# Other token blocks for the first of two MLP layers behind an attention: 512, 256, 512, 512, 512

## Chip, cores and metric

One core of a Trainium2 chip runs the whole program. The metric is the device time in microseconds (us) of one execution; the time of a kernel is the median of its runs. PE is the matmul engine (TensorE), PEld its weight loads, DVE, ACT and POOL are VectorE, ScalarE and GpSimd, and SP issues the DMA transfers (SPq is its queue).

## What is computed

The input is an attention with 4 batches, 8 heads, 576 positions and head size 64, followed by two MLP layers over 2304 tokens, 512 -> 2048 -> 512 each, all in 32-bit floats.

```python
scores = scale * np.matmul(q, k.transpose(0, 1, 3, 2))
bias = -(cum[:, :, :, None] - cum[:, :, None, :])          # cum: running sum of max(s, 0)
scores = np.where(causal, -1e9, scores + np.minimum(bias, 0.0))
attn = softmax(scores)
x = (attn @ v), heads side by side: 2304 x 512
h = x @ w_in;  x = (h * np.clip(h + 3.0, 0.0, 6.0) / 6.0) @ w_out
h = x @ w2_in; out = (h * np.tanh(softplus(h))) @ w2_out
```

## The kernel before

**A planner writes the order.** Every piece of work is a node: engines that may run it, a cost, what it depends on, a due time (its priority) and the buffers that it takes. `Plan.run` (L124) walks through a modelled time, gives each engine the most urgent node that is ready and whose buffers are free, and then emits the instructions in that order. So each engine and SP's one DMA queue run a fixed order. Due times come from the table `T` (L34) in a unit in which one step of a 512-token block is 4: `pos` (L838) is where a step of the MLP stands, 64 for each 512-token block of 16 steps.

**Attention.** Two heads are worked on at a time, a pair. The first 256 positions of a batch are a `small` pair (L582 on): scores L610, score-and-bias minimum on DVE L622, exponential on ACT L629, row sums L637 and L638, scaling L647 and L649, transposes L655, copies L290, probabilities times V L664. Its result is split into a high and a low half and written from PSUM straight into the block of x in SBUF (L673, and L674 on DVE). The other 320 positions are a `unit` (L417 on): scores L486, L493, L501, transposes L532, PV L555, a split into staging tiles (L558 to L561), and a store to DRAM tensors `xs` (L568). `token` (L44) orders the tokens: the four first parts are tokens 0 to 1023, the four second parts are 1024 to 2303, 320 each. `FIRST` (the first parts of batches 0 and 1) runs ahead of everything; the other six parts come at the due times p0 to p5, spread over s0 to s5: first parts of batches 2 and 3, then second parts of batches 0, 1, 2 and 3.

**MLP.** Tokens are cut into five blocks, the same for both layers: 512, 512, 384, 512, 384. A block runs 16 steps f over the hidden size. GEMM1 (L722) is 12 matmuls into one bank: four chunks c of the input size, three products each, because weights and activations are held as a high and a low half. The gate follows (layer 1: ACT L733, DVE L735; layer 2: ACT L740), the split of its result (L290 and DVE L743), and GEMM2 (L755 in layer 1, L760 in layer 2), 12 matmuls per step in layer 1. `T["la"]` and `T["la2"]` say how many steps ahead GEMM1 falls due.

**Weights.** They arrive as 64-bit words and are made into two 32-bit halves by `load_split` (L328): one pass on ACT or DVE (L339, L341), DVE passes L345, L349 and L355, a copy, and a subtraction L365. Layer 1's w_in stays in 16 buffers `win`. w_out is split during block 0, stored to DRAM (`wos`, L390), and read again for each step of the later blocks (L393) into three buffers `wo`. Layer 2's w_out stays in 16 buffers that take the room of the attention's tiles once that is over.

**Blocks of x.** There are two buffers `blk`. Blocks 0 and 1 of layer 1 (tokens 0 to 1023) are taken at the start and filled by the attention from PSUM. Blocks 2 to 4 are loaded from `xs` (L697) once a buffer is free. Layer 1's output is scaled (L778), stored to DRAM tensors `ys` (L782) per block and 128 columns, loaded again by layer 2 (L700) and split (L372).

Of the kernel before, what the change touches and what calls it, by code (L numbers as in the profile page):

```python
# [24 lines left out]
NBLK = len(BLOCKS)  # L25
FIRST = [(0, 0, 2), (1, 0, 2)]
# [219 lines left out]
def tile_attention_moe_moe(ctx, tc, qk1, qk, v1, s, w_in, w_out, w2_in, w2_out, out):  # L246
    nc = tc.nc

    def r(ap):
        return ap.bitcast(F32)  # L250
# [25 lines left out]
    cuml = dr.tile([NB * NH, CTOT - 384], F32, name="cuml")  # L276
    xs = [[dr.tile([P, 2, n], F32, name=f"xs{i}_{c}") for c in range(NCC)] for i, (_, n) in enumerate(BLOCKS)]
    ys = [[dr.tile([P, n], F32, name=f"ys{i}_{c}") for c in range(NCC)] for i, (_, n) in enumerate(BLOCKS)]
    wos = [dr.tile([P, 2, DM], F32, name=f"wos{f}") for f in range(NF)]
# [89 lines left out]
    def split(dep, prio, buf, dst, n):  # L369
        h, l = dst  # L370
        a = add(("ACT", "DVE"), (act(n), v2x(n)), lambda e: copy(e, h(), r(l())), [dep], prio, (), [buf])
        return a, add("DVE", v1x(n), lambda: nc.vector.tensor_tensor(  # L372
            out=l(), in0=r(l()), in1=r(h()), op=ALU.subtract), [a], prio, (), [buf])
# [50 lines left out]
    def unit(b, h, prio, step, dep0, depc, banks):  # L424
# [138 lines left out]
        t0 = token(b, q0)  # L563
        for i, (b0, bn) in enumerate(BLOCKS):
            a, e = max(t0, b0), min(t0 + nq, b0 + bn)
# [6 lines left out]
    def small(b, h, pair, prio, step, dep0, depc, banks, fi, n_c1, n_id):  # L572
# [68 lines left out]
        for g in range(2):  # L641
# [11 lines left out]
            def tr(ps=ps, g=g):  # L653
                for z, o in ((0, 0), (P, P), (2 * P, 2 * P)):
# [13 lines left out]
        i, o = divmod(token(b, 0), 512)  # L668
        c, xb = h // 2, blk[0, i]
# [17 lines left out]

    ys_n = {(i, c): [] for i in range(NBLK) for c in range(NCC)}

    def load_block(layer, i, prio):  # L690
        n = BLOCKS[i][1]
        t = Buf(main_p, "blk", [P, NCC, 2, n], F32R)
        blk[layer, i] = t
        src_n = (xs_n, ys_n)[layer]
        for c in range(NCC):
            if layer == 0:
                ld = add("SP", 0.5, lambda c=c: nc.sync.dma_start(out=r(t.t)[:, c], in_=xs[i][c][:]),  # L697
                         src_n[i, c] + ([first] if c else []), prio, [t] if c == 0 else [], [t], lat=dma(P * n * 8))
            else:
                ld = add("SP", 0.5, lambda c=c: nc.sync.dma_start(out=r(t.t)[:, c, 1, :], in_=ys[i][c][:]),  # L700
                         src_n[i, c] + ([first] if c else []), prio, [t] if c == 0 else [], [t], lat=dma(P * n * 4))
            if c == 0:
                first = ld
            if layer == 0:
                blk_n[layer, i, c] = [ld]
                continue
            blk_n[layer, i, c] = split(ld, prio, t, (lambda c=c: t.t[:, c, 0, :], lambda c=c: t.t[:, c, 1, :]), n)

# [4 lines left out]
    def moe_step(layer, n, t1, t2, hb):  # L713
        i, f = divmod(n, NF)
        N = BLOCKS[i][1]
        x, w = blk[layer, i], win[layer, f]
# [53 lines left out]
    def y_out(layer, i, j, dep, prio):  # L770
        t0, N = BLOCKS[i]
        ps = ypst[layer, i][j]
        if layer == 0:
            t = Buf(main_p, "st", [P, 512], F32)

            def ev(e):
                if e == "ACT":
                    nc.scalar.activation(out=t.t[:, 0:N], in_=ps.t[:, 0:N], func=AF.Copy, scale=1.0 / 6.0)  # L778
                else:
                    nc.vector.tensor_scalar(out=t.t[:, 0:N], in0=ps.t[:, 0:N], scalar1=1.0 / 6.0, scalar2=None, op0=ALU.mult)  # L780
            a = add(("ACT", "DVE"), (actp(N), v1x(N)), ev, [dep], prio, [t], [ps])
# [14 lines left out]
    with tc.manual_schedule():  # L796
# [132 lines left out]
```

## Time and profile before

| | us |
|---|---|
| median of 3 runs | 1002.32 (1001.36 to 1003.06) |
| the profiled execution | 1003.14 |
| its span in the profile | 1001.4 |
| PE busy | 982.1 |
| DVE busy | 462.4 |
| ACT busy | 476.9 |

The span runs from the first to the last instruction in the trace. Matmuls are pipelined, so "busy" counts PE as soon as one is in flight; how close PE is to its pace is read from the start-to-start times of its matmuls. Layer 1 ends and layer 2 begins at about 600 us.

### The profile page before, as it was taken

What the parts mean: (1) busy time and instruction counts of PE and PEld (TensorE: products, weight loads), DVE (VectorE), ACT (ScalarE), POOL (GpSimd) and SP (SyncE); (2) the same over time, 40 slices, a digit from 0 to 9 for tenths busy, and PEclk for the clock granted to TensorE, in tenths of its full rate; (3) what the DMA queues carried; (4) which work ended last, traced back from release to release, by engine and by line L of the source; (5) the groups of instructions that cost most, each with busy time, mean ns of one, the idle gap of its engine ahead of it and who ended that gap; (6) DMA issues with size and microseconds to landing.
All of it is one profiled execution on the core that took longest, in us unless ns stands there. A gap on an engine that the chain in (4) does not pass through costs nothing.

```text
span 1001.4 us, 13786 instructions
## 1 busy us (share of the span) xinstructions
PE 982.1 (98%) x5016; PEld 803.8 (80%) x5016; DVE 462.4 (46%) x1067; ACT 476.9 (48%) x1008; POOL 44.1 (4%) x102
## 2 busy tenths in 40 slices
PE   6899999999999999999999999999999999999998
PEld 3567777777777798888889998888888888888996
DVE  7898887754544455435228879612112112111111
ACT  5887778675665555644226556323123223122222
POOL 1111110100010101000000000000000000000000
PEclk9799999999999999999999999999999999999999
DMA  8676876887566777466237785202001101000101
GB/s 274 199 256 239 275 229 228 276 262 216 168 199 195 233 219 216 138 237 220 85 122 251 254 270 187 84 1 74 1 1 43 43 1 63 1 1 1 43 1 32
DMA packets 60355, 146.05 MB, mean 146 GB/s; under 512 B 8352, under 2 KB 22720, under 8 KB 60288
## 3 DMA queue, kind: packets, MB, share of 16 engines
q1 hardware_dynamic: 60288, 145.17, 44.6%
q8 instruction: 40, 0.66, 0.3%
q14 instruction: 27, 0.22, 0.1%
HBM read 121.84 MB, written 23.31 MB: 145 GB/s over the span
## 4 chain that ended last, share of the span: by engine, by line
PE 95%; DVE 2%; DMA 1%; ACT 1%; issue 0%; SPq 0%; DVEq 0%; ACTq 0%
PE b L722 40%; PE b L755 20%; PE b L760 20%; PE b L486 4%; PE b L555 4%; PE b L532 3%; PE b L610 2%; PE b L664 1%; PE b L655 1%; DMA xs<-st 1%; DMA blk<-xs 0%; PE b L613 0%; DVE g L622 0%; DMA pt<-in_s_dram 0%; DVE win L365 0%
## 5 line engine op out<-in xcount | busy, mean ns | idle before, releaser
L722 PE MATMUL b<-blk,win 128*128 128x512 f32 (+1 forms) x1920 | 505.5, 373 | 0.3 <-DMA blk<-xs 0.3
L722 PEld LDWEIGHTS b<-blk,win 128*128 128x128 f32 x1920 | 347.0, 188 | 58.6 <-issue 6.6
L755 PE MATMUL b<-g,wo 128*128 128x512 f32 (+1 forms) x960 | 258.7, 378 | 0.0
L755 PEld LDWEIGHTS b<-g,wo 128*128 128x128 f32 x960 | 170.3, 188 | 28.6 <-issue 8.4
L743 DVE TENSOR_TENSOR g<-e,g 128x512 fp32r<-128x512 f32 (+1 forms) x120 | 77.2, 644 | 214.4 <-ACT g L290 213.5
L740 ACT ACTIVATE e<-b 128x512 f32<-128x512 f32 (+1 forms) x80 | 44.4, 555 | 249.4 <-PE b L722 249.2
L760 PE MATMUL b<-wo,wo 128*128 128x512 f32 x432 | 122.1, 391 | 0.0
L760 PE MATMUL b<-wo,g 128*128 128x512 f32 x432 | 122.0, 391 | 0.0
L290 ACT ACTIVATE g<-e 128x512 fp32r<-128x512 f32 (+1 forms) x105 | 62.3, 593 | 74.0 <-PE b L755 72.4
L760 PEld LDWEIGHTS b<-wo,g 128*128 128x128 f32 x432 | 80.5, 188 | 13.3 <-DVE g L743 0.3
L760 PEld LDWEIGHTS b<-wo,wo 128*128 128x128 f32 x432 | 80.6, 188 | 12.9
L743 DVE TENSOR_TENSOR wo<-e,wo 128x512 fp32r<-128x512 f32 (+1 forms) x40 | 25.5, 639 | 131.8 <-ACT wo L290 131.6
L735 DVE SCALAR_TENSOR_TENSOR e<-e,b 128x512 f32<-128x512 f32 (+1 forms) x80 | 50.4, 630 | 59.9 <-ACT e L733 59.3
L501 ACT ACTIVATE cb<-cb,nm 128x384 f32<-128x384 f32 (+2 forms) x80 | 54.4, 682 | 29.9 <-DVE nm L493 29.2
L733 ACT ACTIVATE e<-b,three 128x512 f32<-128x512 f32 (+1 forms) x80 | 51.3, 641 | 31.6 <-DVE g L743 15.7
L493 DVE CUSTOM_DVE_ANT_0 cb<-b,cb 128x384 f32<-128x384 f32 (+2 forms) x80 | 44.7, 588 | 29.3 <-PE b L486 24.1
L290 ACT ACTIVATE pt<-b 128x384 f32<-128x384 f32 (+2 forms) x95 | 48.0, 505 | 19.8 <-PE b L532 18.8
L532 PE MATMUL b<-ident,cb 128*128 128x128 f32 x304 | 48.8, 272 | 0.0
L532 PEld LDWEIGHTS b<-ident,cb 128*128 128x128 f32 x304 | 39.0, 140 | 9.2 <-ACT cb L521 0.2
L486 PE MATMUL b<-qk 64*128 64x384 f32 (+2 forms) x288 | 46.2, 364 | 0.0
L355 DVE SCALAR_TENSOR_TENSOR wtmp<-wraw,wtmp 128x512 uint32<-128x512 uint32 x64 | 44.2, 691 | 1.0
L349 DVE SCALAR_TENSOR_TENSOR wtmp<-wraw,wtmp 128x512 uint32<-128x512 uint32 x64 | 44.1, 690 | 1.2
(77 smaller groups left out, 729.8 us busy)
## 6 DMA issues: line engine op xcount, KB each, us to landing
wo<-wos SPq DMA_DIRECT2D x64, 512.0 KB, 4.0
wraw<-in_w_in_dram SPq DMA_DIRECT2D x32, 512.0 KB, 4.6
wraw<-in_w_out_dram SPq DMA_DIRECT2D x32, 512.0 KB, 4.5
cb<-cuml SPq DMA_DIRECT2D x16, 896.0 KB, 7.8
wos<-wo SPq DMA_DIRECT2D x16, 512.0 KB, 5.3
qkr<-in_qk_dram SPq DMA_DIRECT2D x16, 480.0 KB, 3.6
v<-in_v_dram SPq DMA_DIRECT2D x16, 320.0 KB, 6.9
cb<-cums SPq DMA_DIRECT2D x12, 384.0 KB, 4.5
```

The costliest lines, as they stand in the source:

```text
L290: nc.scalar.activation(out=out_, in_=in_, func=AF.Copy)
L486: nc.tensor.matmul(out=ps[g].t[:, 0:w], lhsT=t.t[s_, ka, qo:qo + P], rhs=t.t[s_, kb, nk0 + a:nk0 + e], start=k == 0, stop=k == 2)
L493: nc.vector.tensor_tensor_reduce(out=p.t[:, o:o + w], in0=pb.t[:, 0:w], in1=cb.t[:, o:o + w], scale=-0.125, scalar=(3.0e38 if a == 0 else ...
L501: nc.scalar.activation(out=p.t[:, o:o + w], in_=p.t[:, o:o + w], func=AF.Exp, scale=-1.0, bias=nm.t[:, k:k + 1], accum_out=l.t[:, k:k + 1],)
L532: nc.tensor.transpose(out=ps.t[:, P * z:P * (z + 1)], in_=p.t[:, o:o + P], identity=ident)
L722: nc.tensor.matmul(out=hps.t[:, 0:N], lhsT=w.t[:, a, P * c:P * (c + 1)], rhs=x.t[:, c, b, :], start=(c == 0 and k == 0), stop=(c == NCC - ...
L733: a = add("ACT", actp(N, 1), lambda: nc.scalar.activation(out=e0.t[:, 0:N], in_=hps.t[:, 0:N], func=AF.Relu, bias=three, scale=1.0), [prev ...
L735: a = add("DVE", v1x(N), lambda: nc.vector.scalar_tensor_tensor(out=e0.t[:, 0:N], in0=e0.t[:, 0:N], scalar=6.0, in1=hps.t[:, 0:N], op0=ALU ...
L740: a = add("ACT", actp(N) + 0.15, lambda: nc.scalar.activation(out=e0.t[:, 0:N], in_=hps.t[:, 0:N], func=AF.Mish), [prev], t, [e0], [hps])
L743: gl = add("DVE", v1x(N), lambda: nc.vector.tensor_tensor(out=g.t[:, 1, 0:N], in0=src.t[:, 0:N], in1=r(g.t[:, 0, 0:N]), op=ALU.subtract), ...
L755: nc.tensor.matmul(out=y[j].t[:, 0:N], lhsT=wt.t[:, a, P * j:P * (j + 1)], rhs=g.t[:, b, 0:N], start=(f == 0 and k == 0), stop=(f == NF - ...
L760: nc.tensor.matmul(out=y[j].t, lhsT=g.t[:, a, P * j:P * (j + 1)], rhs=wt.t[:, b, :], start=(f == 0 and k == 0), stop=(f == NF - 1 and k == 2),
```

## The change

Layer 1 gets blocks of its own: 512, 256, 512, 512 and 512 tokens; layer 2 keeps 512, 512, 384, 512 and 384. Block 1 now holds the first part of batch 2 alone. Block 2 (tokens 768 to 1279) holds the first part of batch 3, written from PSUM, and tokens 1024 to 1279, the first 256 of batch 0's second part, loaded from `xs`. `xs` shrinks to what lies behind token 1024 (`LATE`). Block 2's buffer is taken when block 0's is given back, and PV of a first part now waits for the buffer of its block. `ys` is cut at the borders of both layers' blocks, into 8 pieces per 128 columns (32 tensors) rather than 5 (20). The due time of GEMM1 is now that of the step la places before, rather than la times the step's own length. The table of due times is replaced in part.

```diff
-BLOCKS = [(0, 512), (512, 512), (1024, 384), (1408, 512), (1920, 384)]
+BLOCKS = [
+    [(0, 512), (512, 256), (768, 512), (1280, 512), (1792, 512)],
+    [(0, 512), (512, 512), (1024, 384), (1408, 512), (1920, 384)],
+]
+LATE = NB * 256
+CUTS = sorted({b for part in BLOCKS for b, _ in part} | {NT})
+PIECES = list(zip(CUTS, CUTS[1:]))
...
-    sm=3.895, sm2=5.532, w0=5.919, w1=9.308, cum=14.045, wo=0.564, blk0=27.645, blk1=12.97, wo2=44.236,
-    wo2r=11.978, win2=5.088, g=30.578, upre=6.511, uhalf=1.145, upost=3.306, uv=0.304, spre=6.035, shalf=0.728,
-    spost=1.158, pe=5.322, bias=2.302, la=3, la2=2, wp=11.079, p0=-8.796, p1=2.0, p2=2.856,
-    p3=65.354, p4=87.114, p5=119.475, s0=30.881, s1=22.0, s2=23.277, s3=36.84, s4=66.006, s5=29.106,
+    sm=3.895, sm2=5.532, w0=5.919, w1=9.308, cum=11.779, wo=0.159, blk0=19.932, blk1=12.97, wo2=42.769,
+    wo2r=11.978, win2=5.088, g=30.578, upre=2.921, uhalf=1.388, upost=5.963, uv=0.201, spre=4.156, shalf=0.511,
+    spost=1.964, pe=5.322, bias=1.971, la=2, la2=3, wp=16.391, p0=10, p1=67.821, p2=60,
+    p3=91.625, p4=101.026, p5=134.148, s0=45.494, s1=21.005, s2=12.016, s3=23.457, s4=35.969, s5=44.027,
...
-        n_pv = A("PE", 0.73, pv, n_p + [n_v], post, [po], [v])
+        n_pv = A("PE", 0.73, pv, n_p + [n_v, blk_a[bi]], post, [po], [v])
...
+                m = max(0, LATE - b0)
+                ld = add("SP", 0.5, lambda c=c: nc.sync.dma_start(out=r(t.t)[:, c, :, m:], in_=xs[i][c][:]),
+                         [*xs_n[i, c], first], prio, [] if first else [t], [t], lat=dma(P * (n - m) * 8))
...
+            lds = []
+            for k, (a, e) in enumerate(PIECES):
+                if b0 <= a < b0 + n:
+                    lds.append(add("SP", 0.5, lambda c=c, k=k, a=a, e=e: nc.sync.dma_start(
+                        out=r(t.t)[:, c, 1, a - b0:e - b0], in_=ys[k][c][:]),
+                        [*ys_n[k, c], first], prio, [] if first else [t], [t], lat=dma(P * (e - a) * 4)))
+                    first = first or lds[0]
...
-        for i in range(2):
-            blk[0, i] = Buf(main_p, "blk", [P, NCC, 2, 512], F32R)
-            blk_a[i] = add("X", 0.0, lambda: None, [n0], -1e6, [blk[0, i]])
+        for i, (b, n) in enumerate(BLOCKS[0]):
+            if b >= LATE:
+                break
+            blk[0, i] = Buf(main_p, "blk", [P, NCC, 2, n], F32R)
+            blk_a[i] = add("X", 0.0, lambda: None, [n0], -1e6 if i < 2 else 0.0, [blk[0, i]])
...
-            return pos[m] - w * (T["la2"] if layer else T["la"]), pos[m] + w / 2
+            la = T["la2"] if layer else T["la"]
+            return pos[m - la] if m >= la else pos[m] - w * la, pos[m] + w / 2
```

## Rows read from the trace of the kernel before

**Rows 1.** The page: PE's busy tenths in 40 slices, and one costly group (mean ns).
```profile
PE   6899999999999999999999999999999999999998
...
L532 PE MATMUL b<-ident,cb 128*128 128x128 f32 x304 | 48.8, 272 | 0.0
```
**Rows 2.** Waits of PE, whole span: us in total, times, longest.
```profile
PE b L610 <- DMA qkr<-in_qk_dram: 3.6, 1, 3.6
...
PE b L722 <- DMA blk<-xs: 0.3, 1, 0.3
```
**Rows 3.** Timeline of PE, merged matmuls: start, length, line, operands, count.
```profile
655.74 0.84 PE L722 MATMUL b<-blk,win 128*128 128x512 f32 x3
...
661.18 0.84 PE L722 MATMUL b<-blk,win 128*128 128x512 f32 x3
...
328.08 0.56 PE L486 MATMUL b<-qk 128*128 128x288 f32 x3
328.48 0.85 PE L755 MATMUL b<-g,wo 128*128 128x512 f32 x3
```
**Rows 4.** Stretches: busy us of PE, PEld, DVE, ACT, POOL; clock; DMA share; GB/s.
```profile
50.00:75.00 25.00, 24.67 (x119) 15.48 (x119) 23.22 (x70) 21.73 (x64) 3.02 (x6) 1.00 0.78 255
75.00:100.00 25.00, 25.00 (x131) 18.49 (x128) 21.16 (x56) 18.25 (x44) 3.51 (x6) 1.00 0.70 241
...
150.00:200.00 50.00, 50.00 (x268) 37.65 (x267) 38.41 (x90) 37.41 (x80) 5.60 (x10) 1.00 0.75 254
```
**Rows 5.** Groups by shape, 50 to 75 us: count | busy us, mean ns | idle before.
```profile
L722 PE MATMUL b<-blk,win 128*128 128x512 f32 x39 | 12.1, 424 | 0.0
...
L349 DVE SCALAR_TENSOR_TENSOR wtmp<-wraw,wtmp 128x512 uint32<-128x512 uint32 x6 | 4.2, 700 | 0.0
...
L622 DVE CUSTOM_DVE_ANT_0 cb<-b,cb 128x256 f32<-128x256 f32 x7 | 2.9, 414 | 0.0
...
L735 DVE SCALAR_TENSOR_TENSOR e<-e,b 128x512 f32<-128x512 f32 x3 | 2.0, 678 | 0.0
...
L755 PE MATMUL b<-g,wo 128*128 128x512 f32 x6 | 1.6, 407 | 0.0
```
**Rows 6.** Timeline of PE: attention matmuls of both kinds, and what follows them.
```profile
55.57 0.88 PE L664 MATMUL b<-qk 128*64 128x256 f32 x8
56.37 0.97 PE L722 MATMUL b<-blk,win 128*128 128x512 f32 x3
57.41 0.92 PE L610 MATMUL b<-qkr 64*128 64x128 f32 x4
...
254.54 0.49 PE L532 MATMUL b<-ident,cb 128*128 128x128 f32 x3
254.78 0.94 PE L755 MATMUL b<-g,wo 128*128 128x512 f32 x3
...
257.11 2.28 PE L555 MATMUL b<-pt,v 128*64 128x320 f32 x20
```
**Rows 7.** Stretches of L610 alone: busy us (instructions) of PE and PEld, clock, DMA.
```profile
0.00:50.00 50.00, 15.49 (x64) 8.94 (x64) 0.83 0.73 237
50.00:75.00 25.00, 5.52 (x24) 3.10 (x24) 1.00 0.78 255
```
**Rows 8.** Groups of the first 75 us: the last pass of the w_in splits.
```profile
L365 DVE TENSOR_TENSOR win<-wtmp,win 128x512 fp32r<-128x512 f32 x11 | 7.7, 702 | 0.2
```
**Rows 9.** The page's DMA issues: count, KB each, us to landing (two of the groups).
```profile
wo<-wos SPq DMA_DIRECT2D x64, 512.0 KB, 4.0
...
cb<-cuml SPq DMA_DIRECT2D x16, 896.0 KB, 7.8
```
**Rows 10.** A stretch with fewer bytes, columns as in rows 4.
```profile
185.00:210.00 25.00, 25.00 (x138) 18.81 (x137) 17.17 (x38) 16.22 (x33) 2.03 (x4) 1.00 0.75 231
```
**Rows 11.** Waits of SP's queue, whole span: us in total, times, longest.
```profile
SPq L700 <- PE b L722: 161.3, 5, 64.9
```
**Rows 12.** A stretch of L722 alone, columns as in rows 7.
```profile
100.00:185.00 85.00, 31.90 (x109) 19.11 (x109) 1.00 0.76 252
```

More of the change, by code (lines that the diff above doesn't have):

```diff
@@ L276, in tile_attention_moe_moe @@
     cuml = dr.tile([NB * NH, CTOT - 384], F32, name="cuml")
-    xs = [[dr.tile([P, 2, n], F32, name=f"xs{i}_{c}") for c in range(NCC)] for i, (_, n) in enumerate(BLOCKS)]
-    ys = [[dr.tile([P, n], F32, name=f"ys{i}_{c}") for c in range(NCC)] for i, (_, n) in enumerate(BLOCKS)]
+    xs = [[dr.tile([P, 2, min(n, b + n - LATE)], F32, name=f"xs{i}_{c}") if b + n > LATE else None for c in range(NCC)]
+          for i, (b, n) in enumerate(BLOCKS[0])]
+    ys = [[dr.tile([P, e - a], F32, name=f"ys{i}_{c}") for c in range(NCC)] for i, (a, e) in enumerate(PIECES)]
     wos = [dr.tile([P, 2, DM], F32, name=f"wos{f}") for f in range(NF)]
@@ L370, in split @@
         h, l = dst
-        a = add(("ACT", "DVE"), (act(n), v2x(n)), lambda e: copy(e, h(), r(l())), [dep], prio, (), [buf])
+        a = add(("ACT", "DVE"), (act(n), v2x(n)), lambda e: copy(e, h(), r(l())), dep, prio, (), [buf])
         return a, add("DVE", v1x(n), lambda: nc.vector.tensor_tensor(
@@ L563, in unit @@
         t0 = token(b, q0)
-        for i, (b0, bn) in enumerate(BLOCKS):
+        for i, (b0, bn) in enumerate(BLOCKS[0]):
+            b0, bn = max(b0, LATE), b0 + bn - max(b0, LATE)
             a, e = max(t0, b0), min(t0 + nq, b0 + bn)
@@ L659, in small @@
         po = Bank(banks)
+        bi = next(i for i, (b0, bn) in enumerate(BLOCKS[0]) if b0 <= token(b, 0) < b0 + bn)
         def pv():
@@ L665, in pv @@
                                      start=c == 0, stop=c == 1)
[L666 removed]
+        n_pv = A("PE", 0.73, pv, n_p + [n_v, blk_a[bi]], post, [po], [v])
         pt_nodes.append(n_pv)
[L668 removed]
+        i = bi
+        o = token(b, 0) - BLOCKS[0][i][0]
         c, xb = h // 2, blk[0, i]
@@ L686, in units @@
         all_att.extend(pl.nodes[n1:])
-    ys_n = {(i, c): [] for i in range(NBLK) for c in range(NCC)}
+    ys_n = {(k, c): [] for k in range(len(PIECES)) for c in range(NCC)}
     def load_block(layer, i, prio):
[L691 to L694, printed above, removed]
+        b0, n = BLOCKS[layer][i]
+        first = None
+        if layer == 0 and (layer, i) in blk:
+            t, first = blk[layer, i], blk_a[i]
+        else:
+            t = blk[layer, i] = Buf(main_p, "blk", [P, NCC, 2, n], F32R)
         for c in range(NCC):
             if layer == 0:
[L697 to L705, printed above, removed]
-                continue
-            blk_n[layer, i, c] = split(ld, prio, t, (lambda c=c: t.t[:, c, 0, :], lambda c=c: t.t[:, c, 1, :]), n)
+                m = max(0, LATE - b0)
+                ld = add("SP", 0.5, lambda c=c: nc.sync.dma_start(out=r(t.t)[:, c, :, m:], in_=xs[i][c][:]),
+                         [*xs_n[i, c], first], prio, [] if first else [t], [t], lat=dma(P * (n - m) * 8))
+                first = first or ld
+                blk_n.setdefault((layer, i, c), []).append(ld)
+                continue
+            lds = []
[5 more added lines that the diff above has]
+                    first = first or lds[0]
+            blk_n[layer, i, c] = split(lds, prio, t, (lambda c=c: t.t[:, c, 0, :], lambda c=c: t.t[:, c, 1, :]), n)
     ypst = {}
@@ L714, in moe_step @@
         i, f = divmod(n, NF)
-        N = BLOCKS[i][1]
+        N = BLOCKS[layer][i][1]
         x, w = blk[layer, i], win[layer, f]
@@ L770, in y_out @@
     def y_out(layer, i, j, dep, prio):
-        t0, N = BLOCKS[i]
+        t0, N = BLOCKS[layer][i]
         ps = ypst[layer, i][j]
@@ L781, in y_out @@
             a = add(("ACT", "DVE"), (actp(N), v1x(N)), ev, [dep], prio, [t], [ps])
-            ys_n[i, j].append(add("SP", 0.5, lambda: nc.sync.dma_start(out=ys[i][j][:], in_=t.t[:, 0:N]), [a], prio, (), [t],
-                                  lat=dma(P * N * 4)))
+            for k, (b, e) in enumerate(PIECES):
+                if t0 <= b < t0 + N:
+                    ys_n[k, j].append(add("SP", 0.5, lambda k=k, b=b, e=e: nc.sync.dma_start(
+                        out=ys[k][j][:], in_=t.t[:, b - t0:e - t0]), [a], prio, (), [t], lat=dma(P * (e - b) * 4)))
         else:
@@ L841, in tile_attention_moe_moe @@
                 for f in range(NF):
-                    pos.append(pos[-1] + BLOCKS[i][1] / 128.0)
+                    pos.append(pos[-1] + BLOCKS[layer][i][1] / 128.0)
         pos.append(pos[-1])
```

4 lines of the change are left out of this document (2 added, 2 removed).

## The prediction

> **What bounds the kernel now.** The page comes first. PE has matmuls in flight for 982.1 of the 1001.4 us, and of its 40 slices only the first two, 50 us, aren't full [rows 1]. The table of PE's waits names first the operands of the early attention (3.6 us for the first load) and, of the MLP, 0.3 us for one block load [rows 2]; no line of layer 2 stands in it.
>
> A full PE is not a PE at its pace, so next I price the matmuls by their start-to-start times where one kind runs unmixed. Of 512 columns, 24 run from 655.74 to 661.18 us, 227 ns each; three of 288 columns start 0.40 us ahead of the next group, 133 ns each [rows 3]. The straight line through both has 0.42 ns per column: 384 columns make 173 ns, 256 columns 119.
>
> With these prices 50 to 75 us is not full. It holds 39 + 6 MLP matmuls of 512 columns [rows 5], 45 x 0.227 = 10.2 us, and 74 of the attention, the rest of PE's 119 [rows 4]: 24 scores L610 [rows 7] and 50 transposes and PV matmuls. Eight PV matmuls take 0.80 us to the next start and four scores 0.84, their 0.92 less the same tail of 0.08; three transposes take 0.24 [rows 6]. So 24 x 0.21 + 50 x 0.09 = 9.5 us. 25 - 10.2 - 9.5 = 5.3 us are lost though PE looks 99% busy. DVE is busy 23.2 of these 25 us and ACT 21.7; in 75 to 100 us it is 21.2 and 18.3, with PE at 25.0 [rows 4]. So DVE and ACT hold PE back until about 75 us; behind that PE alone sets the time. What is lost ahead of 50 us is the latency of the first eight pairs, whose due times the change keeps.
>
> **The change part by part.**
>
> *Matmul work.* Both layers keep five blocks and 2304 tokens, so neither the count of matmuls nor the sum of columns changes: 227 + 227 + 173 + 227 + 173 before and 4 x 227 + 119 after are both 1027. Cost 0 if the line holds at 256 columns, a form that no row shows. The block has 16 x 24 = 384 of them. From above, one costs no more than the 288 form: 384 x 0.014 = +5 us. From below, transposes of 128 columns follow each other in (0.49 - 0.27) / 2 = 0.11 us, 0.27 being the mean of one [rows 1, 6]: 384 x -0.009 = -4 us. I take the line, because the 288 form, 32 columns away, lies on it.
>
> At 512 columns the weight load is fully covered: 227 ns are the 213 of 512 columns at the 2.4 GHz level plus 14 [rows 3]. The Trainium skill, "TensorE: Matmul & The Clock Gate", Part 3, section "The mechanism", says that a weight load overlaps running matmuls only where the row group differs, and its section "LDWEIGHTS (loading the stationary operand)" has 107 ns for 128 columns; by both, an estimated 320 ns per matmul of 512. The trace disagrees.
>
> *What block 1 no longer needs.* It needs batch 2's first part alone. Batch 3's goes to block 2, whose buffer comes free with block 0's last GEMM1. The due times say the same: batch 2's first part p0 from -8.8 to 10, batch 3's p1 from 2 to 67.8, batch 0's second part p2 from 2.9 to 60. A pair has eight L610 matmuls. The 64 of batches 0 and 1 lie before 50 us, so the 24 of 50 to 75 us are three pairs of batches 2 and 3 [rows 7]. One costs PE 8 x 0.21 + 6 x 0.08 + 8 x 0.10 = 3.0 us and DVE also about 3.0: four L622, two of them of 0.41, with a read each, row sums, scaling and L674 [rows 5, 6]. With two of the three pushed behind 75 us, 6 us of DVE and of PE come free.
>
> A step of block 0 is 24 x 0.227 = 5.45 us of PE. On DVE its w_out split has three passes of about 0.69 and one of 0.44, 2.5 us, and its gate two of 0.68, 1.4 us [rows 5]: 3.9 DVE us as long as w_in splits are in stock, and 11 are done by 75 us [rows 8]. So 6 DVE us feed 1.5 steps, 8.4 us of PE, in place of 6.0: 2.4 us recovered. Bounds: 0 if the steps wait for something else, 5.3 if the whole loss goes. I take 2.5. Late next is the stock of w_in: from about 60 us 22 splits x 2.5, 16 gates x 1.4 and four pairs x 3.0 make 89 us of DVE against 87 + 12 + 6 (mixing) = 105 us of PE, a load of 85%. DVE carries that in 75 to 100 us with PE full [rows 4], so it costs nothing; without that cover, each per cent of DVE that is missing costs 1 us.
>
> *Mixing.* A group of three MLP matmuls behind transposes is 0.94 us long where a plain one has 0.84 [rows 3, 6]: each return from attention costs about 0.1 us. Some 200 such returns stand in the trace behind 60 us. The attention groups stay the same, their neighbours don't; a tenth more or fewer is 2 us. I take 0, bounds -2 and +2; layer 1's shorter lookahead lies inside.
>
> *The added wait.* PV of batch 3's first part depends on block 2's buffer, freed by block 0's last GEMM1. That matmul is earlier in PE's own order, so nothing behind PV on PE waits longer, and the copies on ACT and DVE follow PV as now: 0. Its price is that four pairs, four units of batch 0's second part and block 1's 16 short steps share one stretch.
>
> *Transfers in that stretch.* w_out is read anew for each step, 16 x 512 KB. A unit loads 1984 KB, of which 896 are the largest piece of its bias rows; a pair loads 768; xs takes 8 x 160 and block 2's half 4 x 256 (of the page's nine groups two are shown [rows 9]). Together 22 MB. PE's own time there is 384 x 0.119 = 46 us, pairs 4 x 3.0 = 12, units 4 x 6.3 = 25 (2.2 of PV; 2.4 of scores; 19 transposes [rows 3, 6]) and 5 of mixing: 88 us, so 250 GB/s are asked. 150 to 200 us moved 254 with PE full [rows 4]: 0 us, at the edge. At 231 GB/s, seen too [rows 10], it takes 95 us: +7. SP issues in order and `wo` has three buffers, so one late load holds those behind it.
>
> *The rest.* `ys` in 32 tensors rather than 20 adds 24 issues on SP, where layer 2's block loads already wait 161 us for their buffers [rows 11]: 0; uncovered, the 0.3 us that a late block load costs now [rows 2], five times. Layer 2's blocks and the tail stay, and PE doesn't wait in layer 2, so la2 is 0 as well.
>
> Sum: -2.5 us from the front and 0 from all else, with bounds of -11 and +14 that don't fall all on one side. The profiled execution took 1003.1 us, 1.7 around its span; the median, 1002.3, is 0.8 lower. So 1000.6 for such an execution and 999.8 as a median.
>
> **The rivals.**
>
> *Given back.* DVE has 32 splits to do before block 0 ends in either kernel. If PE loses later in block 0 what it gained before 75 us, or the mixing gets 2 us dearer, the time is 1002.3. For it: a DVE load of 85% in a fixed order. Against it: 75 to 100 us carries that load. It is also the time if the new order doesn't start block 0 denser at all. Chance 0.24.
>
> *Starved in block 1.* A step of 2.9 us of PE draws 512 KB, beside eight pieces of attention. It decides below 243 GB/s (22 MB in 90.5 us), where the loss is as large as the gain; at 231, 7 - 2.5 gives 1006.8. For it: 185 to 210 us moved no more [rows 10]. Against it: PE was full there, so that stretch didn't ask for more. Chance 0.18.
>
> *A 256-column matmul is no faster than one of 288.* 5 - 2.5: 1004.8. For it: nothing narrower stands in the trace in this form. Against: the line. Chance 0.07. With its weight load uncovered it would take 0.12 + 0.11 us, 384 x 0.11 = 42 us more: 1042. The 227 ns speak against that; chance 0.01. It is what the rule of the Trainium skill above would bring.
>
> *The deferral pays more.* All 5.3 us come back and the groups pack 1 us better: 996. Chance 0.14. That leaves 0.36 for the forecast.
>
> **How the numbers follow.** The forecast, 999.8, is the likeliest. A measurement of this kernel can tell about 0.2%, 2 us, so faster means 1000.3 or less: 0.29 of the forecast's 0.36, and the 0.14, make 0.43. Slower than 1004.3 are 0.16 of starved, 0.08 of the dearer matmul and 0.03 of given back: 0.27. Within stay 0.07 + 0.21 + 0.02 = 0.30. The range, 994 to 1007, leaves out the far ends alone.
>
> **What would show it.** Right: in 50 to 75 us more than 45 MLP matmuls and fewer than 24 L610, DVE still over 0.85; block 0's GEMM1, now through at about 185 us with 109 of its 192 matmuls behind 100 us [rows 12], through well before; PE full from there on and layer 2 as long as now. Wrong: PE waits on `wo`, `xs` or `cb` around the 256-token block; DVE over 0.9 past 100 us with PE idle; groups of three 256-column matmuls over 0.38 us apart.

## The result, and the profile after

The change made the kernel slower: 1011.1 us median (1006.91 to 1012.49, five runs) beside 1002.5 (1001.36 to 1003.23, five runs) for the kernel before, a ratio of 1.0079, interval 1.0064 to 1.0094. The prediction was faster, 999.8 us within 994 to 1007: sign and range were both wrong. The profiled execution of the kernel after took 1012.49 us, with a span of 1010.7.

The page of the kernel after, PE's busy tenths and its granted clock in 40 slices of 25.3 us, answers [rows 1]:

```profile
PE   6899999999999999899999999999999999999998
...
PEclk9799999999999999799999999999999999999999
```

One slice in the middle, 404 to 429 us, is not full, and its clock is down too. Before, every slice between the first two and the last was full. Stretches of the kernel after (columns as in [rows 4]):

```profile
50.00:75.00 25.00, 24.31 (x118) 15.88 (x117) 22.03 (x61) 18.33 (x51) 3.00 (x6) 0.91 0.70 232
75.00:100.00 25.00, 25.00 (x114) 20.71 (x113) 21.95 (x40) 12.31 (x21) 0.00 (x0) 1.00 0.62 225
...
175.00:200.00 25.00, 25.00 (x193) 21.89 (x191) 12.10 (x41) 14.80 (x39) 0.81 (x2) 1.00 0.83 269
200.00:225.00 25.00, 25.00 (x201) 21.97 (x200) 13.43 (x48) 14.99 (x40) 2.73 (x6) 1.00 0.71 227
...
400.00:425.00 25.00, 21.30 (x110) 14.09 (x110) 9.48 (x27) 13.96 (x30) 2.73 (x8) 0.80 0.78 239
```

and the last of them in the kernel before:

```profile
400.00:425.00 25.00, 25.00 (x169) 21.61 (x167) 12.46 (x37) 16.07 (x38) 1.41 (x4) 1.00 0.46 138
```

From 400 to 425 us PE starts 110 matmuls where it started 169, idles 3.7 us, and runs at a mean granted clock of 0.80. No engine is near its limit there: DVE 9.5 of 25 us, ACT 14.0.

**How the loss is counted.** Busy time says little of a pipelined PE, so I price every matmul as in the prediction: those of the MLP at N/2.4 + 14 ns for N columns (the line through [rows 3]), those of the attention at the mean gap that their kind has in dense stretches. The loss at a time t is t minus the prices of all that started before. It is worked out from the traces' start times and is no row of a profile. Both kernels do matmuls of the same total price, so a difference that stays to the end is a difference of the span. Transposes that an experiment adds are priced at nothing. In us:

| loss up to | 50 | 75 | 100 | 150 | 400 | 425 | 450 | end |
|---|---|---|---|---|---|---|---|---|
| before | 27.3 | 32.3 | 33.9 | 37.1 | 52.2 | 53.8 | 54.9 | 57.0 |
| after | 28.3 | 34.0 | 34.0 | 37.0 | 52.8 | 62.3 | 63.9 | 66.4 |

At 400 us the two are within 0.6 us of each other. The next 25 us cost 9.5 us instead of 1.6, and the rest is alike. So the result has two parts: a hole at 400 us, and the absence of the gain forecast for the first 100 us.

**The hole.** Timeline of PE in the kernel after (start, length, line, operands, count, and in brackets the idle time ahead with what ended it):

```profile
400.56 2.27 PE L562 MATMUL b<-pt,v 128*64 128x320 f32 x20
403.93 0.55 PE L539 MATMUL b<-ident,cb 128*128 128x128 f32 x3 [1.09 <-ACT cb L528]
404.90 2.91 PE L539 MATMUL b<-ident,cb 128*128 128x128 f32 x13 [0.42 <-DVE st L568]
408.07 0.90 PE L539 MATMUL b<-ident,cb 128*128 128x128 f32 x3 [0.26 <-ACT pt L297]
410.70 4.32 PE L562 MATMUL b<-pt,v 128*64 128x320 f32 x20 [1.73 <-ACT pt L297]
414.95 2.27 PE L737 MATMUL b<-blk,win 128*128 128x512 f32 x6
```

SP's queue in the same time, and one step of the chain that ended last:

```profile
403.36 3.06 SPq L576 DMA_DIRECT2D xs<-st  x4
...
409.32 0.32 SPq L710 DMA_DIRECT2D blk<-xs  x1
```

```profile
405.03 4.05 DMA xs<-st
```

Read together: PV (L562) at 400.56 is that of the last pair of batch 2's second part. Its first 128 tokens, 1664 to 1791, are the end of block 3, chunk 3. The result is split on ACT and DVE until 404.8 and stored to `xs`; once block 3's pieces have landed it is loaded again, from 409.32, and that load lands 3.6 us later, at 412.9 (an issue of SP between 409.3 and 409.6 us: KB, us to landing):

```profile
blk<-xs SPq DMA_DIRECT2D x1, 512.0 KB, 3.6
```

GEMM1 (L737) uses it at 414.95, 12 us behind the end of PV and 2 behind the landing, because the next pair's PV stands ahead of it in PE's order. PE has nothing else in these 12 us but that pair's chain, in which each transpose waits for ACT. The chain is held up by a store as well: ACT copies block 2's output into a staging tile, waits 0.88 us for one to come free from a store to `xs` (the one of 4.05 us above), and copies the last transposes only then.

```profile
409.18 1.09 ACT L793 ACTIVATE st<-b 128x512 f32<-128x512 f32 x2 [0.88 <-DMA xs<-st]
```

In the hole the granted clock falls to 1.2 GHz (406.1 to 416.3 us), so that the second PV takes 4.32 us rather than 2.27. The table of PE's waits doesn't name the transfer at all; behind 140 us its entries, the largest being

```profile
PE b L562 <- ACT pt L297: 1.7, 1, 1.7
PE b L539 <- ACT cb L528: 1.1, 1, 1.1
```

add up to 4.0 us, because PE is kept half busy by latency-bound work.

In the kernel before the last pair of batch 2 comes later, and still in time. Its PV runs at 424.95 us, block 3's first GEMM1 at 435.40, and the first on chunk 3 at 441.57:

```profile
424.95 2.28 PE L555 MATMUL b<-pt,v 128*64 128x320 f32 x20
...
435.40 0.94 PE L722 MATMUL b<-blk,win 128*128 128x512 f32 x3
...
441.57 0.86 PE L722 MATMUL b<-blk,win 128*128 128x512 f32 x3
```

SP's queue there: four stores mark a unit whose tokens lie in two blocks, and the load is the last of block 3's four. It takes 3.5 us and lands at 435.0, so chunk 3 is there 6.5 us before PE uses it.

```profile
427.73 2.79 SPq L568 DMA_DIRECT2D xs<-st  x4
431.51 0.32 SPq L697 DMA_DIRECT2D blk<-xs  x1
```

After, block 3's first GEMM1, on chunks whose data are there, stands at 387.56 us, 13 us ahead of the start of that PV. So PV comes 24 us earlier than before, but block 3 starts 48 us earlier: only 512 + 256 + 512 = 1280 tokens of the MLP stand ahead of it rather than 1408, and, since second parts start later (the first unit's PV is at 170 us instead of 104), 11 of their PVs instead of 15. Before, block 3 starts 8.2 us behind the end of that PV; after, 15.3 us ahead of it. Yet it still needs all pairs of batch 2's second part.

**The front.** The second stretch answers [rows 7] and the counts of [rows 5]; L618 (scores, L610 before), then GEMM1 L737, then GEMM2 L770, each alone from 50 to 75 us:

```profile
50.00:75.00 25.00, 3.68 (x16) 2.07 (x16) 0.91 0.70 232
...
50.00:75.00 25.00, 13.24 (x43) 7.49 (x42) 0.91 0.70 232
...
50.00:75.00 25.00, 1.70 (x6) 1.13 (x6) 0.91 0.70 232
```

16 scores instead of 24 and 49 MLP matmuls instead of 45: the deferral happened. But the clock of this stretch is 0.91, not 1.00. Smaller windows, first of after and then of before (columns as in [rows 4]):

```profile
45.00:50.00 5.00, 5.00 (x14) 2.99 (x14) 4.15 (x16) 3.90 (x12) 0.00 (x0) 0.50 0.23 77
50.00:55.00 5.00, 5.00 (x23) 3.15 (x23) 2.53 (x8) 2.84 (x10) 0.76 (x2) 0.55 0.56 189
```

```profile
45.00:50.00 5.00, 3.55 (x27) 2.46 (x28) 4.96 (x23) 4.77 (x17) 0.00 (x0) 1.00 0.64 198
50.00:55.00 5.00, 4.74 (x25) 2.59 (x24) 4.93 (x13) 5.00 (x17) 0.95 (x2) 1.00 0.76 252
```

PE is granted 1.2 GHz once in the kernel before, from 22.7 to 39.8 us. After, it is twice, from 23.8 to 34.0 and again from 44.2 to 54.5. In the second stretch PE itself becomes the bound: always busy, with DVE down to 2.5 of 5 us. On the timeline three 512-column matmuls take 1.65 us there ([rows 6] has 0.97 for three):

```profile
44.09 0.79 PE L663 MATMUL b<-ident,cb 128*128 128x128 f32 x3 [1.84 <-ACT cb L655]
...
48.79 1.65 PE L737 MATMUL b<-blk,win 128*128 128x512 f32 x3
```

Two theories go to the chip. **Hole:** block 3 starts before its last tokens are there, by the border and the new due times. **Front:** the replaced small due times (`spre`, `shalf`, `spost`, `bias`, `cum`, `wo`) thin out PE around 44 us, the clock falls again, and that takes what the deferral gives. Against them stand the rivals of the prediction (transfers in block 1, dearer 256-column matmuls) and that the deferral itself, or the altered code, costs the time.

### The profile page after: what moved, and what is told of

Same layout as the page of the kernel before. It is cut to its first block, busy times and chain, and to the rows that moved or that the text cites. A ratio compares the mean times of both kernels' runs of the same rounds, so it can differ in the third digit from the quotient of the medians.

```text
span 1010.7 us, 13892 instructions
## 1 busy us (share of the span) xinstructions
PE 988.8 (98%) x5016; PEld 794.8 (79%) x5016; DVE 471.3 (47%) x1103; ACT 461.5 (46%) x972; POOL 41.8 (4%) x102
## 4 chain that ended last, share of the span: by engine, by line
PE 93%; DVE 2%; DMA 2%; ACT 2%; issue 1%; POOL 0%; SPq 0%; ACTq 0%; POOLq 0%
PE b L737 39%; PE b L775 20%; PE b L770 19%; PE b L493 4%; PE b L562 4%; PE b L539 3%; PE b L618 2%; PE b L663 1%; PE b L673 1%; DMA wraw<-in_w_in_dram 1%; DMA g<-cums 0%; DMA xs<-st 0%; PE b L621 0%; DVE wtmp L362 0%; DVE win L372 0%
## 5 line engine op out<-in xcount | busy, mean ns | idle before, releaser
L737 PE MATMUL b<-blk,win 128*128 128x512 f32 (+2 forms) x1920 | 503.0, 374 | 0.6 <-ACT blk L297 0.4
L737 PEld LDWEIGHTS b<-blk,win 128*128 128x128 f32 x1920 | 344.8, 189 | 68.3 <-issue 8.7
L770 PE MATMUL b<-g,wo 128*128 128x512 f32 (+1 forms) x960 | 257.8, 377 | 0.0
L770 PEld LDWEIGHTS b<-g,wo 128*128 128x128 f32 x960 | 166.1, 188 | 32.8 <-issue 7.3
L758 DVE TENSOR_TENSOR g<-e,g 128x512 fp32r<-128x512 f32 (+2 forms) x120 | 76.7, 639 | 202.0 <-ACT g L297 201.5
L297 ACT ACTIVATE g<-e 128x512 fp32r<-128x512 f32 (+2 forms) x95 | 57.0, 600 | 51.8 <-PE b L770 28.5
L748 ACT ACTIVATE e<-b,three 128x512 f32<-128x512 f32 (+1 forms) x80 | 51.4, 642 | 52.1 <-PE b L737 51.6
L508 ACT ACTIVATE cb<-cb,nm 128x384 f32<-128x384 f32 (+2 forms) x80 | 54.5, 683 | 29.3 <-DVE nm L500 28.3
L346 ACT ACTIVATE wtmp<-wraw 128x512 f32<-128x512 f32 x59 | 39.3, 668 | 32.4 <-DMA wraw<-in_w_out_dram 12.8
L539 PEld LDWEIGHTS b<-ident,cb 128*128 128x128 f32 x304 | 38.1, 143 | 12.7 <-ACT cb L528 1.5
L356 DVE SCALAR_TENSOR_TENSOR wtmp<-wraw,wtmp 128x512 uint32<-128x512 uint32 x64 | 44.2, 690 | 1.0
```

The source lines that it names most:

```text
L297: nc.scalar.activation(out=out_, in_=in_, func=AF.Copy)
L508: nc.scalar.activation(out=p.t[:, o:o + w], in_=p.t[:, o:o + w], func=AF.Exp, scale=-1.0, bias=nm.t[:, k:k + 1], accum_out=l.t[:, k:k + 1],)
L539: nc.tensor.transpose(out=ps.t[:, P * z:P * (z + 1)], in_=p.t[:, o:o + P], identity=ident)
L737: nc.tensor.matmul(out=hps.t[:, 0:N], lhsT=w.t[:, a, P * c:P * (c + 1)], rhs=x.t[:, c, b, :], start=(c == 0 and k == 0), stop=(c == NCC - ...
L748: a = add("ACT", actp(N, 1), lambda: nc.scalar.activation(out=e0.t[:, 0:N], in_=hps.t[:, 0:N], func=AF.Relu, bias=three, scale=1.0), [prev ...
L758: gl = add("DVE", v1x(N), lambda: nc.vector.tensor_tensor(out=g.t[:, 1, 0:N], in0=src.t[:, 0:N], in1=r(g.t[:, 0, 0:N]), op=ALU.subtract), ...
```

## Experiments

Kernels that share a value of "before" ran beside each other on one chip. Intervals are 95%.

**The kernel after once more**, unedited, to see what of its trace repeats.

> The changed kernel once more, on the chip of the three runs that follow. Theory 'deadline' (the second part of batch 2 must be through PV, its store to xs and its load before block 3 can start, and block 3 now starts 128 tokens of MLP earlier): 1007 to 1012 us, with one hole of PE of some 10 us ahead of the first GEMM1 of block 3 and nothing else lost against the kernel before. Theory 'clock' (what is lost is what PE does at 1.2 GHz at about 44 to 54 and 406 to 416 us): the time goes with the stretches at half clock, and a run without them is near 1002.

1010.25 us (4 runs) beside 1002.37: 1.0079 [1.0064, 1.0094]. The hole is there again, at full clock this time (first a stretch, columns as in [rows 4], then PE's timeline, then a step of the chain that ended last):

```profile
400.00:425.00 25.00, 21.60 (x130) 14.88 (x129) 12.46 (x34) 17.35 (x38) 3.50 (x8) 1.00 0.80 241
```

```profile
410.04 2.28 PE L562 MATMUL b<-pt,v 128*64 128x320 f32 x20 [1.09 <-ACT pt L297]
412.56 1.65 PE L737 MATMUL b<-blk,win 128*128 128x512 f32 x6 [0.25 <-DMA blk<-xs]
```

```profile
408.64 3.88 DMA blk<-xs
```

5.9 us are lost from 400 to 425, beside 9.5 in the first profile, where the second PV and the six GEMM1 behind it took 2.7 us more at 1.2 GHz. Here PE does wait for the load: it lands at 412.52, and GEMM1 starts 0.04 us later. So the hole stands without the low clock. Nor is a full clock enough for 1002 us: among the five runs of the kernel after, one with a mean granted clock of 0.999 took 1012.14. The half clock of the front repeats at 44.1 to 54.3 us.

**Block 3 without batch 2's data.** This kernel leaves out batch 2's part of block 3 and fills the room from batch 1's tiles.

```diff
 in unit(), the store of one piece to xs
+            if (b, i) == (2, 3):
+                continue
+            if (b, i) == (1, 3):
+                # batch 1's pair also fills the room: columns 384 to 511
+                ... dma_start(out=xs[i][h // 2][:, k, 384:512], in_=r(x.t[:, 0:128]))
```

> The changed kernel, but the last 128 tokens of block 3, which belong to batch 2, are written into xs from batch 1's tiles, so that block 3 waits for nothing of batch 2 (the values of these 128 tokens are wrong; the number of stores, loads and matmuls is the same). Theory 'deadline': the hole goes, some 9 us less than the changed kernel, 1000 to 1003. Theory 'clock', or any theory by which the deferral costs DVE, ACT or DMA time elsewhere: within 3 us of the changed kernel.

1007.63 us (4 runs) beside 1002.37: 1.0056 [1.0038, 1.0074]. The hole is gone (a stretch with the columns of [rows 4]), 1.5 us are lost there, beside 1.6 in the kernel before:

```profile
400.00:425.00 25.00, 25.00 (x147) 18.46 (x146) 11.39 (x31) 16.78 (x36) 4.28 (x8) 1.00 0.81 235
```

But the time falls by 2.6 us only, within the 3 us of the other theory's range, so the time alone doesn't decide. Its trace shows the hole gone and a worse front: half clock from 35.0 to 55.4 us and a loss of 36.1 at 100 us, 1.7 more than in the repeat above.

**The last 128 tokens of block 3 without DRAM.** Block 3's buffer is taken early and PV's result written into it from PSUM, as first parts do.

```diff
+DIRECT = (2, 3)
+            if (b, i) == DIRECT and a < e:
+                ... copy(en, xb.t[:, c, 0, o:o + e - a], po.t[:, a - t0:e - t0])  # deps n_pv, blk_a[i]
+                ... nc.vector.tensor_tensor(out=xb.t[:, c, 1, ...], in0=po.t[...], op=ALU.subtract)
+                continue
```

> The changed kernel, but batch 2's 128 tokens of block 3 go from PSUM straight into block 3's buffer (a copy and a subtraction of 128 columns per pair), without the store to xs and the load. The last pair of batch 2 still has to pass PV ahead of block 3. If the round trip through DRAM makes the hole (store, landing, load: 403 to 415 us in the trace): 1000 to 1003. If the attention of that pair is itself too late: 1005 to 1008, with half of the hole left. If neither: as the changed kernel, 1007 to 1012.

1006.48 us (1002.28 to 1008.62, 8 runs) beside 1002.37: 1.0033 [1.0012, 1.0053]. Nothing is left out here, and GEMM1 (now L747) goes on 1.4 us behind the end of that PV (L563):

```profile
400.79 2.28 PE L563 MATMUL b<-pt,v 128*64 128x320 f32 x20
403.00 1.66 PE L780 MATMUL b<-g,wo 128*128 128x512 f32 x6
404.49 0.84 PE L747 MATMUL b<-blk,win 128*128 128x512 f32 x3
```

1.3 us are lost in these 25 us. The time lies in the second range, yet no half of the hole is left; what stays is the front: 38.1 at 100 us, with three half-clock stretches, in a profiled execution of 1008.58 us, 2.1 above the median. Its eight runs spread over 6 us and go with the mean granted clock: 0.983 gave 1008.6 and 0.992 gave 1002.5, correlation -0.92.

**The border alone**, in the kernel before's order: blocks 0 and 1 and the whole table of due times are those of before, only block 3 begins at 1280.

```diff
-    [(0, 512), (512, 256), (768, 512), (1280, 512), (1792, 512)],
+    [(0, 512), (512, 512), (1024, 256), (1280, 512), (1792, 512)],
     T: as in the kernel before
```

> The kernel before with its own due times and its own first two blocks, but blocks 2 to 4 of layer 1 are 256, 512 and 512 tokens, so that block 3 begins at token 1280 as in the changed kernel and needs batch 2 there (ys cut as in the changed code). Theory 'deadline': slower by 7 to 12 us, with the hole at block 3's start and the front as before. Theories that blame the front (block 1 of 256 tokens, the moved first parts, the new due times): within 2 us of the kernel before.

1009.96 us (4 runs) beside 1002.37: 1.0077 [1.0062, 1.0092], the whole loss of the change from one border. Here PE waits for the load itself:

```profile
427.58 3.59 PE L562 MATMUL b<-pt,v 128*64 128x320 f32 x20 [0.58 <-ACT pt L297]
...
433.39 5.98 PE L737 MATMUL b<-blk,win 128*128 128x512 f32 x18 [2.22 <-DMA blk<-xs]
```

It loses 10.1 us from 400 to 450, where before lost 2.7. Block 3's first GEMM1 is at 411.11 us here and the last PV that it needs ends at 419.3. So the border suffices; with the deferral on top the hole moves but does not grow.

**Batch 2's first part back at its old due time**, on top of the direct write: is the deferral what spoils the front?

```diff
-    p0=10, s0=45.494
+    p0=-8.796, s0=30.881
```

> The kernel a_direct (no hole ahead of block 3; 1006.5 us, its profile loses some 4 us more than the kernel before in the first 75 us), with the due times of batch 2's first part put back to those of before (p0 = -8.796, s0 = 30.881). Theory 'sparse front' (with batch 2's pairs deferred, PE has too little to do at 40 to 60 us, is granted 1.2 GHz there and works through the last pairs of batch 1 at half pace): the front is as before, no half clock after 45 us, 1002 to 1004 us. If the front's loss comes from something else in the new table (the small pairs' other due times, the bias, the lookahead): 1005 to 1008 as a_direct.

1005.38 us (10 runs) beside 1002.95: 1.0027 [1.0014, 1.0040], the front still at 37.5 by 100 us and half clock in four stretches, the last of them at 61.8 to 68.6. The deferral of batch 2 is not the cause; that of batch 3 (p1) stays in this kernel.

**PE kept at work in the front**, on top of the direct write: five transposes of the identity, whose result is overwritten, ahead of each of the first pairs' 16 transpose groups, 80 in all.

```diff
             def tr(ps=ps, g=g):
+                for _ in range(5 if fi else 0):
+                    nc.tensor.transpose(out=ps.t[:, 0:P], in_=ident, identity=ident)
```

> The kernel a_direct with five idle transposes of the identity ahead of each group of transposes in the first parts of batches 0 and 1 (80 more matmuls of 0.11 us at full clock; they wait for nothing but their bank, and the groups behind them overwrite what they write). PE so has work while it waits for ACT. Theory 'the clock itself costs the front its time': no stretch at 1.2 GHz after 40 us, 1001 to 1004 us. Theory 'DVE and ACT bound the front, and the low clock only shows that PE waits': 1006 to 1009, no gain or a small loss from the added work.

1002.47 us (1002.0 to 1004.21, 10 runs) beside 1002.95: 1.0001 [0.9991, 1.0010]. Work was added and the time fell by 4 us against the direct write alone (which ran on another chip; beside the kernel before the two are at 1.0033 and 1.0001). The clock is now full where it was half, and the runs lie within 2.2 us (first the direct write, then this kernel; columns as in [rows 4]):

```profile
45.00:50.00 5.00, 3.94 (x15) 2.27 (x12) 4.85 (x20) 3.70 (x12) 0.00 (x0) 0.50 0.25 75
```

```profile
45.00:50.00 5.00, 5.00 (x31) 3.27 (x32) 4.87 (x20) 4.56 (x16) 0.00 (x0) 1.00 0.29 99
50.00:75.00 25.00, 24.69 (x135) 17.34 (x135) 23.64 (x64) 19.23 (x52) 3.08 (x6) 1.00 0.72 235
```

The loss at 100 us is 32.6 instead of 38.1.

**The same transposes in the kernel before.** The edit is the one above.

> The kernel before with the same idle transposes in the first parts of batches 0 and 1. It has one stretch at 1.2 GHz, 22.7 to 39.8 us. Theory 'the clock itself costs': 999 to 1001.5 us and no such stretch, or a shorter one. Theory 'DVE and ACT bound the front': 1002 to 1005.

1003.04 us (10 runs) beside 1002.95: 1.0006 [0.9995, 1.0016]. Its half clock shrinks from 17 us to 3.4 (25.4 to 28.8) and nothing is gained; the loss at 100 us stays 33.9: there PE waits for DVE and ACT at either clock. So in this order the cure gives nothing back. That half clock costs nothing here is not shown: the added transposes are work of their own, and among the 31 unedited runs beside them the eight at a mean granted clock of 0.994 or more took 1001.7 us, the 22 at 0.991 or less 1003.2 (medians).

**The changed code with the blocks and due times of before.**

```diff
-    [(0, 512), (512, 256), (768, 512), (1280, 512), (1792, 512)],
+    [(0, 512), (512, 512), (1024, 384), (1408, 512), (1920, 384)],
     T: as in the kernel before
```

> The changed code with the blocks and the due times of the kernel before: what is left of the change are the 32 instead of 24 pieces of ys at these borders' count (here 20, as before), the due time of GEMM1 taken from the step la before, and the split of the block loads. All theories: 1001 to 1004 us, no difference; if it is slower by more than 3, the changed code itself costs and not the blocks or the due times.

1003.04 us (10 runs) beside 1002.95: 1.0000 [0.9991, 1.0010]. The altered code as such costs nothing. What these borders don't exercise is left untested by it: `ys` in 32 tensors (there are 20 here) and PV's wait for a buffer that is taken late.

**The transposes in the kernel after**, with its hole left in: what is the front's share?

> The changed kernel with the idle transposes of a_direct_warm in the first parts of batches 0 and 1, and nothing else: the hole ahead of block 3 stays. If the loss is the sum of the hole and of the front at 1.2 GHz, this takes the front's part alone: 1006 to 1008 us, some 3 to 4 less than the changed kernel, with the front as in a_direct_warm (32 to 33 us lost by 100 us) and the hole of 6 to 9 us still there. If the hole's cost depends on the front, it goes below 1004 or stays at 1010.

1007.38 us (5 runs) beside 1003.18: 1.0050 [1.0033, 1.0067], some 3 us better than the kernel after. The profiled execution is the slowest of the five, 1010.69 us; its front saves 0.7 us (33.3 beside 34.0 at 100 us), so how the 3 us divide is not shown. The hole stays, 8.6 us from 400 to 425:

```profile
400.00:425.00 25.00, 20.41 (x116) 13.29 (x112) 10.76 (x27) 15.61 (x33) 2.76 (x8) 0.93 0.78 226
```

The clock is only down for 3.4 us here (410.0 to 413.4), and the hole is still 8.6 us. With the repeat above, which has the hole at full clock: the drop of the clock follows the hole and lengthens it, but is not its cause.

**The small due times of before**, on top of the direct write, without added transposes: the deferral with the old front.

```diff
-    cum=11.779, wo=0.159, spre=4.156, shalf=0.511, spost=1.964, bias=1.971
+    cum=14.045, wo=0.564, spre=6.035, shalf=0.728, spost=1.158, bias=2.302
```

> The kernel a_direct with the due times that order the first parts (spre, shalf, spost, bias, cum, wo) put back to those of before; batch 2's first part stays deferred (p0 = 10, s0 = 45.5). Theory 'the small due times make PE's early work sparse': the front is as before (33 to 35 us lost by 100 us, one stretch at 1.2 GHz that ends at about 40 us), 1002 to 1004 us. Theory 'the deferral of batch 2 makes it sparse': as a_direct, 1005 to 1008.

1005.3 us (10 runs) beside 1003.18: 1.0018 [1.0009, 1.0027]. The front is as in the first theory, the time as in the second. The loss is 31.9 at 100 us and 34.2 at 150, 2.0 and 2.9 better than before, with one stretch of half clock as before. Then 4.2 us go between 150 and 175, as block 1 begins. PE's waits name two of that place, a split of w_out and a piece of the block from DVE:

```profile
PE b L747 <- DVE blk L302: 0.9, 1, 0.9
PE b L780 <- DVE wo L373: 0.4, 1, 0.4
```

**Both cures with other due times**: the direct write and the transposes with nine due times altered (`g`, `upost`, `spre`, `bias`, `p0`, `p2`, `p5`, `s2`, `s4`).

> A try at a better kernel: a_direct_warm (no round trip ahead of block 3, idle transposes in the front) with nine due times moved so that the planner's own order has no gap of over 0.8 us behind 47 us (p5 143.3, p2 51.7, s2 13.7, s4 32.9, spre 3.4, bias 2.06, upost 6.35, g 24.2, p0 10.4). Both theories: as a_direct_warm or up to 2 us less, 1000 to 1002.5 us.

1005.13 us (10 runs) beside 1003.18: 1.0021 [1.0012, 1.0031]. Above the range of both theories. The clock was full from 27.3 to 68.2 us, but the loss is 36.9 at 100 us: PE waits for DVE and ACT in this order, from 65 to 70 us for 2.3 of 5. A full clock doesn't mend an order that starves PE.

**The old small due times and others for the rest**: the direct write with the small due times of before, and nine more altered.

```diff
-    blk0=19.932, uhalf=1.388, uv=0.201, p1=67.821, p2=60,     p4=101.026, p5=134.148, s4=35.969, s5=44.027
+    blk0=22.66,  uhalf=1.463, uv=0.155, p1=60.334, p2=51.971, p4=86.043,  p5=144.139, s4=34.121, s5=47.387
```

> The kernel a_direct_front (first parts ordered as in the kernel before, batch 2's first part deferred, no round trip ahead of block 3) with nine due times of the later attention moved so that the planner's own order has no gap at the start of block 1, where a_direct_front lost 4.2 us in 150 to 175 us (p1 60.3, p2 52.0, p4 86.0, p5 144.1, s4 34.1, s5 47.4, uhalf 1.46, uv 0.155, blk0 22.7). If the deferral is worth the 2 to 3 us that a_direct_front's front shows by 150 us, and nothing takes them back: 1000 to 1001.5 us, faster than the kernel before by 1.5 to 3. If they are always taken back at the start of blocks 1 and 2: 1002.5 to 1005.

1001.2 us (998.67 to 1002.53, 12 runs) beside 1003.02 (17 runs): 0.998 [0.997, 0.999]. This is faster than both kernels, although the clock is half for 17 us of the front (24.4 to 34.6 and 38.1 to 44.9). The deferral is kept (32.4 at 100 us, 34.8 at 150), block 1 begins at 152 us without a gap (36.3 at 175), and the stretch of the hole is full:

```profile
400.00:425.00 25.00, 25.00 (x132) 19.37 (x133) 15.83 (x40) 17.91 (x39) 3.66 (x7) 1.00 0.57 176
```

The losses of five of these kernels, in us:

| loss up to | 75 | 100 | 150 | 400 | 425 | end |
|---|---|---|---|---|---|---|
| direct write | 37.9 | 38.1 | | 56.8 | 58.1 | 62.4 |
| direct write, transposes | 32.4 | 32.6 | | 51.0 | | 56.4 |
| after, transposes | 33.1 | 33.3 | | 52.1 | 60.7 | 64.5 |
| direct write, old small due times | 31.8 | 31.9 | 34.2 | 52.6 | | 59.0 |
| the same, other due times (fastest) | 32.5 | 32.4 | 34.8 | 49.6 | 50.8 | 54.9 |

## Why the prediction was wrong, point by point

**The step that failed: "behind that PE alone sets the time", and with it "The rest".** The sum has no term for whether the data of a block of layer 1 that comes through `xs` are there when PE comes to it. "The rest" prices late loads for layer 2 alone, at the 0.3 us that one costs now [rows 2], "five times" if uncovered, and puts 0 into the sum. That 0.3 us was block 2's; block 3's last load had 6.5 us to spare, which no table of waits shows. The step that belonged there was a comparison of two places for every block: where PE is when the block's GEMM1 falls due, and where the PV of its last token stands. Block 3's first GEMM1 is 8.2 us behind the end of that PV before and 15.3 us ahead of it after. The border alone brings 16.4 of these 23.5 us (8.2 us ahead in the experiment on it): the block starts after 1280 tokens of MLP instead of 1408 while it still needs 128 tokens of each of batch 2's pairs. The due times bring the rest: they move this PV forward too, but the block's start by more, as second parts give way (p2 from 2.9 to 60). Measured, the step is worth 7.6 us by the border alone, and 7.9 of the 9.4 us by which the two profiled executions differ (9.5 - 1.6), some of that by the low clock in the hole. The direct write and the kernel without that data show the cause from the other side: the loss in the stretch falls to 1.3 and 1.5 us.

**A second step that failed: "whose due times the change keeps".** What is lost ahead of 50 us was taken as unchanged since the first eight pairs stay where they are. Where a pair starts stays, but `spre`, `shalf`, `spost`, `bias` and `cum` place the work inside it, and those are replaced. The result is the second stretch of half clock. With those due times put back (loss at 100 us 38.1 to 31.9), or with the clock held up by idle transposes (38.1 to 32.6), it goes; the 38.1 is that of the execution of 1008.58 us. In the two profiled executions of the kernel after the front came out at 34.0 and 34.4, so that it ate the gain and no more; in the direct write it cost 4 us beyond.

**The forecast's mechanism held in part.** Fewer scores in 50 to 75 us, more MLP matmuls, block 0's GEMM1 through at 152 instead of 184 us: each of these signs came. Recovered are 2.0 us by 100 us and 2.9 by 150 with the old small due times, where 2.5 was forecast. That the sizes agree is partly luck: by 75 us only 0.5 are recovered (31.8 beside 32.3), and 1.5 come in 75 to 100 us, where the prediction took PE to be at its pace and the kernel before loses 1.6. "PE full from there on" did not come, and no sign was set at block 3, where the loss arose. The gain is realised only where the front is kept and the start of block 1 is supplied: 0 in the kernel after, 1.5 and 2.3 us at these two places in the fastest kernel.

**A 256-column matmul** follows the line. Timeline of PE in block 1 of the kernel after:

```profile
184.55 0.52 PE L737 MATMUL b<-blk,win 128*128 128x256 f32 x3
184.91 0.52 PE L770 MATMUL b<-g,wo 128*128 128x256 f32 x3
185.27 0.52 PE L737 MATMUL b<-blk,win 128*128 128x256 f32 x3
```

0.36 us for three, 120 ns each, beside 119 predicted. So the rival at 1004.8 falls, and with it the one at 1042: the rule of the Trainium skill, "TensorE: Matmul & The Clock Gate", Part 3, "The mechanism", that a weight load overlaps only where the row group differs, is not what this stream of 128-row loads shows. The same section's first paragraph leaves a second case open, a load into a background weight buffer; no run here tells which case this is.

**Starved in block 1** didn't happen either: 269 and 227 GB/s in 175 to 225 us with PE full, and the loss from 150 to 200 is 3.3 us beside 3.0. That the transfers were "at the edge" is right in so far as 269 was reached.

**Given back** describes one experiment, not the kernel after: with the old small due times, 4.2 us are lost again as block 1 begins. PE's waits there point to DVE's order, and the fastest kernel has the same deferral without the loss; which of its altered due times does it is not shown.

**The added wait, `ys` in 32 tensors, layer 2 and the tail at 0** were right as far as the traces show: no wait of a first part's PV for its block stands among PE's waits in the kernel after, the changed code with old blocks and due times is at 1.0000, and from 450 us to the end the loss grows by 2.5 us after and 2.1 before.

**What stays open.** Which feature of the order makes the granted clock fall at 44 us in one order and not in another was not isolated: the runs show what PE did around it, sparse and waiting for ACT, and that added matmuls avoid it. Why one and the same kernel differs by up to 6 us between executions is tied to the clock by the correlation alone, and in the kernel after not even by that (-0.14 over five runs, with the one at 0.999 that took 1012.14 us). And the nine altered due times of the fastest kernel were not tried one by one.

## What to carry to other kernels

When a tiling border moves, list for every tile the last producer that it needs and compare its place with the consumer's, before and after; slack that the old order had is in no table of waits, and a table of waits hides a hole that the engine half fills with other, latency-bound work. When a table of due times is replaced together with a tiling, price each of its entries as a change of its own: here the border was worth +7.6 us of time, and the deferral and the small due times -2 to -3 and +2 to +6 us of loss in the first 100 to 150 us. And look at the granted clock of each stretch next to who waits: keeping it up gained 4 us in an order where PE had work in stock, and nothing in one where it waited for DVE and ACT.

## What the hardware showed that was not expected

- A round trip through DRAM between PV and the GEMM1 that uses it took 9.0 us in the repeat of the kernel after, where nothing hid it: 5.0 from the end of PV (403.6) to the issue of the load, with split and stores, and 3.9 to its landing. In the first profile it was 10.0 us to the landing, and in the border experiment 14.0, of which 6.3 passed before ACT copied PV's result (425.65), held up by its order and by a staging tile that an earlier store still used.
- Adding 80 idle transposes went with a time 4 us shorter: the granted clock of 45 to 50 us rose from 0.50 to 1.00, and the ten runs lay within 2.2 us instead of 6.3 us for eight. The same 80 in the kernel before gained nothing.
- In the direct write 0.001 of mean granted clock went with 0.75 us of time over eight runs, more than twice the 0.35 us of the kernel before over 31. So how the time goes with the clock differs from order to order; why is not shown.
